# FFT, expert feed-forward and top-1 routing on one core: gates moved from the token loop to the expert tiles

## The chip, the cores and the metric

The kernel runs on 1 core of one Trainium2 chip. The metric is the device time of one execution in microseconds (us), a median over runs.

## What is computed

```python
def reference(x, w1, w2, w3, w_out, expert_emb, tau, e_w1, e_w2):
    X = np.fft.fft(np.fft.fft(x, axis=1), axis=2).real      # x: 8 x 3072 x 256
    t = X.reshape(8 * 3072, 256)
    t = ((t @ w1) * (t @ w2)) @ w3 @ w_out                   # 256 -> 1024 -> 256
    tn = t / (norm(t) + 1e-6)
    logits = tn @ (emb / (norm(emb) + 1e-6)).T / tau         # 8 experts
    e = argmax(logits)
    p = exp(logits - max(logits)); p /= p.sum() + 1e-9
    out[token] = p[e] * (relu(t @ e_w1[e]) @ e_w2[e])        # the chosen expert only
```

p[e] is the gate. At the maximum the exponential is 1, so the gate is one over the sum of the exponentials.

## The kernel before

All matrix products are made from high and low halves: `split` (L110) writes the high half with a ScalarE copy and the low half as source minus high half, on VectorE or GpSimd; three products of halves stand for one. Names with h and l at the end (`jh`, `jl`; `eh`, `el`; `hh`, `hl`) are such halves.

The program has three stretches. The first (to about 315 us) makes the transform of x and folds the constant matrices. The second, `mid` (L714), runs over 24 chunks of 512 columns, each column standing for two tokens (sum and difference), 1024 tokens a chunk; a 25th round is the tail. A chunk has eight steps i. In a step, `stage_b` (L767) makes one block of 128 features of the running chunk c: 13 matmuls of 128x512 into the PSUM tiles `p` and `q`, then the copies and elementwise products `ps`, `a`, `b`, `g`. `just` (L801) splits one block of 128 tokens of the chunk before into `jh` (ScalarE) and `jl` (GpSimd), and `stage_c` (L808) makes its 24 matmuls of 128x264 into one PSUM tile `pc`: 256 features and 8 logits. There is one `pc`; ScalarE copies it into the chunk's row tile `xs` (L815), and the next block's first matmul waits for that copy. After it ScalarE squares and sums the 256 features (L817, tile `jk`).

In step 1 `choose` (L822) works on the eight blocks of the chunk before that one: maximum, the square root of the sum of squares by shifts and three rounds of reciprocal and two multiply-adds (`norm_of`, L127), difference `df`, argmin `mi`, one-hot `oh`, the exponential `ex` on ScalarE (L851), and then the gate and the token number into the row's columns 256 and 257 (L855, L856), over the logits:

```python
        nc.scalar.activation(out=ex, in_=df, func=AF.Exp)
        nc.vector.reciprocal(out=xs[:, 0:nt, D], in_=su)
        nc.vector.tensor_copy(xs[:, 0:nt, D + 1].bitcast(I32), tok[:, t0:t0 + nt])
```

In step 2 `place` ranks the tokens by expert with matmuls, and from step 3 on `scatter` (L879) writes each block's rows of 258 words into the DRAM array `dx`, ordered by expert, with an indirect DMA that GpSimd issues. In every second step `presplit` (L887) takes one of 64 pieces of the experts' weights: SyncE loads `et`, ScalarE and VectorE split it, SyncE stores `eh` and `el` to DRAM; its pool has two buffers for each tile. The next chunk's columns `ru` and `rv` are split in step 5 (`uh`, `ul`, `vh`, `vl`).

The third stretch, `experts` (L1111), runs over up to 103 tiles of 256 rows of `dx`; 100 are sure to run. `turn` transposes a tile into `xh`, `xl`; `up` makes four hidden blocks `pd` and splits them (`hh` on ScalarE L1087, `hl` on VectorE L1088); `down` and `gated` (L1093) make two output blocks `po`, scale them by the gate in the row (`o`, L1102, ScalarE) and scatter them to the token's row of the output (GpSimd, L1103). The first tile is made in the tail, in pieces between the last blocks (`lead_tiles`). A scheduler places the instructions of each engine within a stretch; in `experts` SyncE's order is the program's.

Of the kernel before, what the change touches and what calls it, by code (L numbers as in the profile page):

```python
# [8 lines left out]
F32 = mybir.dt.float32  # L9
# [15 lines left out]
XW = 258  # L25
# [34 lines left out]
def fourier_experts(  # L60
# [110 lines left out]
    def open_p1():  # L171
# [52 lines left out]
    with ExitStack() as c2:  # L224
        c2.enter_context(tc.manual_schedule(engines={mybir.EngineType.SP}))
        experts(nc, tc, c2, p1["w"], p1["xs"], ident, run, t_g, eg, lead, dx, dex, out)
# [487 lines left out]
def mid(  # L714
# [44 lines left out]
    nc.gpsimd.memset(zrow[:, D + 1:D + 2].bitcast(I32), N)  # L759
# [40 lines left out]

    def just(gt, j, lo_eng=nc.gpsimd):  # L801
# [3 lines left out]
        split(h, l, src, lo_eng=lo_eng)  # L805
        return h, l

    def stage_c(hl, xs, ss, j, tag="c"):  # L808
# [13 lines left out]
    def choose(xs, ss, nt, t0, masked, j0=0):  # L822
        xs, ss = xs[:, j0:j0 + nt], ss[:, j0:j0 + nt]
# [5 lines left out]
        nrm = small("nrm", 1)[:, :nt]  # L829
        norm_of(nrm, ss[:, :nt], ro, 128, nt, f"n{nt}")  # L830
        nc.vector.tensor_scalar_add(nrm, nrm, 1e-6)
        inv = small("inv", 1)[:, :nt]
        nc.vector.reciprocal(out=inv, in_=nrm)
# [15 lines left out]
        ex = small("ex")[:, :nt]  # L849
        nc.vector.tensor_tensor(out=df, in0=df, in1=inv.unsqueeze(2).to_broadcast(sh), op=ALU.mult)  # L850
        nc.scalar.activation(out=ex, in_=df, func=AF.Exp)  # L851
        su = small("su", 1)[:, :nt]
# [34 lines left out]
    def presplit(n):  # L887
# [7 lines left out]
        split(h, l, t)  # L895
# [36 lines left out]
    def mini_out(hl):  # L932
        xs = xsp.tile([128, 8, 264], F32, tag="xs", name="xsm")
        ss = ro.tile([128, 8], F32, tag="ss", name="ssm")
        stage_c(hl, xs, ss, 0)
        idx = place(*choose(xs, ss, 1, NCH * 8, True))
# [30 lines left out]
    def lead_tiles():  # L967
        w = p1["w"].rearrange("p (a c) -> p a c", c=2048)
        for x in p1["xs"][:INLINE]:
# [3 lines left out]
            transposed(nc, x, identr, ps, h, l)  # L973
            yield
# [6 lines left out]
            for a in range(2):  # L981
                ps = pp.tile([128, D], F32, tag=f"b{a}", name="lo")
                o = wk.tile([128, D], F32, tag=f"a{a}", name="lout")
                gated(nc, tc, w, hs, a, x, ps, o, out)
# [7 lines left out]
    for c in range(NCH + 1):  # L992
# [5 lines left out]
        if gprev is not None:  # L998
            lo_eng = nc.gpsimd if c < NCH else nc.vector
            if c == NCH:  # L1000
                w0 = p1["w"].rearrange("p (a c) -> p a c", c=2048)
                p1["xs"] = [p1["x"][:, 0:2, :], p1["x"][:, 2:4, :]] + [
                    p1["raw"].tile([128, 2, XW], F32R, tag=t, name="xl") for t in ("ru", "rv")
                ]
                for g, t in enumerate(p1["xs"]):
                    nc.sync.dma_start(
                        out=t.bitcast(F32),
# [5 lines left out]
            xs = xsp.tile([128, 8, 264], F32, tag="xs", name="xs")  # L1013
            ss = ro.tile([128, 8], F32, tag="ss", name="ss")
        masked = (c - 2) % (H // CH) == 0
        for i in range(8):
            if c < NCH:
# [6 lines left out]
                late = (hl, xs, ss, i) if gprev is not None else None  # L1024
                if c == 1 and i == 1:
                    mini_out(hm)
                if pend is not None:
                    if i == CHOOSE:
                        sel = choose(*pend, 8, (c - 2) * 8, masked)
# [29 lines left out]
        pend = (xs, ss) if gprev is not None else None  # L1059
# [33 lines left out]
def gated(nc, tc, w, hs, a, x, ps, o, out):  # L1093
# [3 lines left out]
    for f in range(FT):  # L1097
# [13 lines left out]
def experts(nc, tc, ctx, w0, x0, ident, run, t_g, eg, lead, dx, dex, out):  # L1111
# [6 lines left out]
    xp = pool("xx", LOOK + 2)  # L1118
    wp = pool("xw", 1)
# [20 lines left out]
    nc.gpsimd.memset(zrow[:, D + 1:D + 2].bitcast(I32), N)  # L1140
# [29 lines left out]
    def load_x(g):  # L1170
        r = nc.sync.value_load(entry(1, g), min_val=0, max_val=ROWS - TS)
        t = xp.tile([128, 2, XW], F32R, tag="x", name="x")
        nc.sync.dma_start(out=t.bitcast(F32), in_=dx[bass.ds(r, TS), :].rearrange("(a p) c -> p a c", p=128))
        return t

    xts, ths = {}, {}

    def turn(p):
# [3 lines left out]
        ths[p] = (h, l)  # L1182

# [46 lines left out]
    def table(a, b):  # L1230
        n = b - a
        sh = [1, n, E]
        cm = cp.tile(sh, F32, name=f"cm{a}")
# [9 lines left out]
        rw = cp.tile([1, n], F32, name=f"rw{a}")  # L1243
# [6 lines left out]
        ch = cp.tile([1, n], F32, name=f"ch{a}")  # L1250
# [154 lines left out]
```

## Time and profile before

| | us |
|---|---|
| three runs | 2750.07, 2757.14, 2759.6 |
| median | 2757.14 |
| the profiled execution | 2768.9 |
| its span | 2767.2 |
| its mean granted TensorE clock | 0.976 |
| PE, PEld, DVE busy | 2602.1, 2441.5, 1690.8 |
| ACT, POOL busy | 1049.5, 1078.0 |

The profile names the engines PE (TensorE's matmuls), PEld (its weight loads), DVE (VectorE), ACT (ScalarE), POOL (GpSimd) and SP (SyncE). Shares over the whole span mix the three stretches: VectorE's 1690.8 us lie mostly in the first two, and from about 1610 us on it is busy under a third of the time. So a stretch is looked at by itself, cut where a chunk's first copy of `p` stands in ScalarE's rows. The profiled execution lies 11.8 us above the median of the runs.

### The profile page before, as it was taken

What the parts mean: (1) busy time and instruction counts of PE and PEld (TensorE: products, weight loads), DVE (VectorE), ACT (ScalarE), POOL (GpSimd) and SP (SyncE); (2) the same over time, 40 slices, a digit from 0 to 9 for tenths busy, and PEclk for the clock granted to TensorE, in tenths of its full rate; (3) what the DMA queues carried; (4) which work ended last, traced back from release to release, by engine and by line L of the source; (5) the groups of instructions that cost most, each with busy time, mean ns of one, the idle gap of its engine ahead of it and who ended that gap; (6) DMA issues with size and microseconds to landing.
All of it is one profiled execution on the core that took longest, in us unless ns stands there. A gap on an engine that the chain in (4) does not pass through costs nothing.

```text
span 2767.2 us, 48866 instructions
## 1 busy us (share of the span) xinstructions
PE 2602.1 (94%) x18661; PEld 2441.5 (88%) x18661; DVE 1690.8 (61%) x3325; ACT 1049.5 (38%) x2069; POOL 1078.0 (39%) x748
## 2 busy tenths in 40 slices
PE   4988789999999999999999999999999999999998
PEld 3888677877888888888888899999999999999998
DVE  8999389999888878888888852222222222222222
ACT  3554234444434334434344433333333333333332
POOL 5465345565566555565565421111111111111111
PEclk7999899999999999999999999999999999999999
DMA  6766625455211011011010264111111422111110
GB/s 247 242 220 201 199 92 184 164 173 191 73 41 41 28 43 39 28 43 39 28 43 20 108 267 169 47 47 47 47 47 47 163 104 104 47 47 47 47 47 21
DMA packets 114249, 265.07 MB, mean 96 GB/s; under 512 B 16843, under 2 KB 55929, under 8 KB 109148
## 3 DMA queue, kind: packets, MB, share of 16 engines
q1 hardware_dynamic: 84670, 195.58, 21.5%
q0 software_dynamic: 19440, 51.35, 5.2%
q10 hardware_dynamic: 9902, 14.98, 1.5%
q8 instruction: 148, 2.42, 0.4%
q14 instruction: 89, 0.73, 0.1%
HBM read 521.17 MB, written 106.77 MB: 227 GB/s over the span
## 4 chain that ended last, share of the span: by engine, by line
issue 39%; PE 27%; DVE 17%; POOL 11%; DMA 3%; ACT 2%; POOLq 0%; SPq 0%; DVEq 0%; ACTq 0%
PE pc L122 14%; POOL out L1103 7%; PE p L122 6%; PE q L122 5%; DVE b L796 2%; DVE g L799 2%; POOL vl L115 2%; DMA et<-in 2%; DVE a L796 2%; PE acc L122 1%; DVE ps L781 1%; DVE el L115 1%; ACT jh L112 1%; DVE nrm L139 1%; POOL z L504 1%
## 5 line engine op out<-in xcount | busy, mean ns | idle before, releaser
L1088 DVE SCALAR_TENSOR_TENSOR hl<-pd,hh 128x512 fp32r<-128x512 f32 x396 | 273.8, 691 | 783.5 <-ACT hh L1087 752.6
L115 POOL TENSOR_TENSOR jl<-g,jh 128x1024 fp32r<-128x1024 f32 x184 | 443.0, 2409 | 393.9 <-ACT jh L112 330.2
L1103 POOL DMA_INDIRECT out<-o,x x192 | 187.3, 976 | 916.0 <-ACT o L1102 897.2
L122 PE MATMUL pc<-wh,jh 128*128 128x264 f32 x1536 | 449.9, 293 | 53.1 <-ACT xs L815 50.4
L122 PE MATMUL pc<-wh,jl 128*128 128x264 f32 x1536 | 444.1, 289 | 4.1 <-POOL jl L115 4.0
L122 PE MATMUL pc<-wl,jh 128*128 128x264 f32 x1536 | 442.7, 288 | 0.0
L1084 PE MATMUL pd<-xh,wt 128*128 128x256 f32 x2400 | 431.4, 278 | 0.0
L1100 PE MATMUL po<-wt,hh 128*128 128x256 f32 x2400 | 423.9, 280 | 0.0
L112 ACT ACTIVATE jh<-g 128x1024 fp32r<-128x1024 f32 x192 | 203.2, 1059 | 476.4 <-PE pc L122 350.7
L1084 PEld LDWEIGHTS pd<-xh,wt 128*128 128x128 f32 x2400 | 370.0, 188 | 0.0
L122 PEld LDWEIGHTS pc<-wh,jh 128*128 128x128 f32 x1536 | 296.4, 193 | 82.4 <-ACT xs L815 73.3
L1087 ACT ACTIVATE hh<-pd 128x512 fp32r<-128x512 f32 x396 | 236.7, 598 | 339.8 <-PE pd L1084 339.8
L1100 PEld LDWEIGHTS po<-wt,hh 128*128 128x128 f32 x2400 | 364.4, 188 | 0.0
L1100 PE MATMUL po<-wt,hl 128*128 128x256 f32 x1200 | 334.1, 278 | 0.0
L1084 PE MATMUL pd<-xl,wt 128*128 128x256 f32 x1200 | 333.9, 278 | 0.0
L122 PE MATMUL q<-vh,wc 128*128 128x512 f32 x768 | 308.0, 403 | 17.2 <-ACT a L794 10.6
L122 PE MATMUL p<-uh,wc 128*128 128x512 f32 x768 | 308.1, 402 | 3.7 <-DVE ps L781 3.6
L122 PEld LDWEIGHTS pc<-wl,jh 128*128 128x128 f32 x1536 | 296.9, 193 | 5.8
L122 PEld LDWEIGHTS pc<-wh,jl 128*128 128x128 f32 x1536 | 295.9, 193 | 5.6 <-POOL jl L115 5.4
L796 DVE TENSOR_TENSOR b<-ps,q 128x512 f32<-128x512 f32 x384 | 249.0, 688 | 33.9 <-ACT ps L785 20.3
L880 POOL DMA_INDIRECT dx<-xs,idx x192 | 192.5, 1003 | 154.3 <-DVE idx L876 82.0
L799 DVE TENSOR_TENSOR g<-a,b 128x512 f32<-128x512 f32 x384 | 247.6, 679 | 7.7 <-POOL a L796 7.5
(336 smaller groups left out, 5073.4 us busy)
## 6 DMA issues: line engine op xcount, KB each, us to landing
wt<-dex SPq DMA_DIRECT2D x75, 4096.0 KB
wc<-dex SPq DMA_DIRECT2D x22, 4096.0 KB
x<-dx SPq DMA_DIRECT2D x96, 258.0 KB
xt<-in SPq DMA_DIRECT2D x24, 1028.0 KB
et<-in SPq DMA_DIRECT2D x64, 256.0 KB
dex<-eh SPq DMA_DIRECT2D x64, 256.0 KB
dex<-el SPq DMA_DIRECT2D x64, 256.0 KB
raw<-in SPq DMA_DIRECT2D x28, 512.0 KB
```

The source lines that it names most:

```text
L112: nc.scalar.activation(out=hi, in_=src, func=AF.Copy)
L115: (lo_eng or nc.vector).tensor_tensor(out=lo, in0=src, in1=hi.bitcast(F32), op=ALU.subtract)
L122: nc.tensor.matmul(ps, lhsT=lh, rhs=rh, start=first and i == 0, stop=last and i == n - 1)
L139: nc.vector.scalar_tensor_tensor(out=n_, in0=n_, scalar=0.5, in1=t, op0=ALU.mult, op1=ALU.add)
L796: eng.tensor_tensor(out=t, in0=ps, in1=q, op=o)
L799: nc.vector.tensor_tensor(out=gt[sg][:, f, :], in0=ab[0][sg], in1=ab[1][sg], op=ALU.mult)
L880: i = nc.gpsimd.indirect_dma_start(out=dx, out_offset=bass.IndirectOffsetOnAxis(ap=idx[:, j if k is None else k:][:, 0:1], axis=0), in_=xs ...
L1084: nc.tensor.matmul(ps[:, a, :], lhsT=w[:, lh, o:o + 128], rhs=rh[:, k, :], start=i == 0, stop=i == 5)
L1087: nc.scalar.activation(out=hh[:, sl, :], in_=ps, func=AF.Relu)
L1088: nc.vector.scalar_tensor_tensor(out=hl[:, sl, :], in0=ps, scalar=0.0, in1=hh[:, sl, :].bitcast(F32), op0=ALU.max, op1=ALU.subtract)
L1100: nc.tensor.matmul(ps, lhsT=lh[:, f, sl], rhs=w[:, rh, c:c + D], start=i == 0, stop=i == 3 * FT - 1)
L1103: ins = nc.gpsimd.indirect_dma_start(out=out, out_offset=bass.IndirectOffsetOnAxis(ap=x[:, a, D + 1:D + 2].bitcast(U32), axis=0), in_=o, i ...
```

## The change

The scattered row keeps the logits. It grows from 258 to 265 words: 256 features, 8 logits, and the token number in word 264 (`TK`). The squares leave `stage_c`; the norm, the exponential and the gate leave `choose`. The token number is written by one operation that reads `mi` (always above -1, so the comparison adds 0). A new function `gates` computes a tile's gates from the rows in `turn` (and for the first tile in `lead_tiles`), and `gated` scales by its result. `presplit`'s low half goes to GpSimd. Each scatter is issued behind the `jl` of its step. `table` gives its temporary tiles common tags.

```diff
-XW = 258
+XW = 265
+XP = 272
+TK = 264
...
+    low = [None]
     def just(gt, j, lo_eng=nc.gpsimd):
-        split(h, l, src, lo_eng=lo_eng)
+        low[0] = split(h, l, src, lo_eng=lo_eng).ins
...
-        nc.scalar.activation(out=xs[:, j, :], in_=pc, func=AF.Copy)
-        jk = wk.tile([128, D], F32, tag="jk", name="jk")
-        nc.scalar.activation(out=jk, in_=xs[:, j, 0:D], func=AF.Square, accum_out=ss[:, j:j + 1])
+        nc.scalar.activation(out=xs[:, j, 0:TK], in_=pc, func=AF.Copy)
...
-        norm_of(nrm, ss[:, :nt], ro, 128, nt, f"n{nt}")
-        nc.vector.tensor_scalar_add(nrm, nrm, 1e-6)
-        nc.vector.reciprocal(out=inv, in_=nrm)
...
-        nc.vector.tensor_tensor(out=df, in0=df, in1=inv.unsqueeze(2).to_broadcast(sh), op=ALU.mult)
-        nc.scalar.activation(out=ex, in_=df, func=AF.Exp)
-        nc.vector.tensor_reduce(out=su, in_=ex, axis=AX.X, op=ALU.add)
-        nc.vector.tensor_scalar_add(su, su, 1e-9)
-        nc.vector.reciprocal(out=xs[:, 0:nt, D], in_=su)
-        nc.vector.tensor_copy(xs[:, 0:nt, D + 1].bitcast(I32), tok[:, t0:t0 + nt])
+        nc.vector.scalar_tensor_tensor(
+            out=xs[:, 0:nt, TK].bitcast(I32), in0=mi, scalar=-1.0, in1=tok[:, t0:t0 + nt],
+            op0=ALU.is_lt, op1=ALU.add
+        )
...
-        split(h, l, t)
+        split(h, l, t, lo_eng=nc.gpsimd)
...
-                            scatter(pend[0], idx, j)
+                            with tc.issue_after(low[0]):
+                                scatter(pend, idx, j)
...
+def gates(nc, pool, junk, x, norm_of):
+    sh = [128, 2, E]
+    new = lambda nm, *w: pool.tile([128, *w], F32, tag="g" + nm, name="g" + nm)
+    ss, nrm, mx, inv, gate = (new(nm, 2) for nm in ("ss", "nrm", "mx", "inv", "gate"))
+    for a in range(2):
+        nc.scalar.activation(out=junk, in_=x[:, a, 0:D].bitcast(F32), func=AF.Square, accum_out=ss[:, a:a + 1])
+    lg = x[:, :, D:D + E].bitcast(F32)
+    nc.vector.tensor_reduce(out=mx, in_=lg, axis=AX.X, op=ALU.max)
+    norm_of(nrm, ss, pool, 128, 2, "gn")
+    nc.vector.tensor_scalar_add(nrm, nrm, 1e-6)
+    nc.vector.reciprocal(out=inv, in_=nrm)
+    df = new("df", 2, E)
+    nc.vector.tensor_tensor(out=df, in0=lg, in1=mx.unsqueeze(2).to_broadcast(sh), op=ALU.subtract)
+    nc.vector.tensor_tensor(out=df, in0=df, in1=inv.unsqueeze(2).to_broadcast(sh), op=ALU.mult)
+    ex = new("ex", 2, E)
+    nc.scalar.activation(out=ex, in_=df, func=AF.Exp)
+    nc.vector.tensor_reduce(out=gate, in_=ex, axis=AX.X, op=ALU.add)
+    nc.vector.tensor_scalar_add(gate, gate, 1e-9)
+    nc.vector.reciprocal(out=gate, in_=gate)
+    return gate
...
-    nc.scalar.activation(out=o, in_=ps, func=AF.Copy, scale=x[:, a, D:D + 1].bitcast(F32))
+    nc.scalar.activation(out=o, in_=ps, func=AF.Copy, scale=gate[:, a:a + 1])
...
+    gtp = pool("xg", 3)
...
         ths[p] = (h, l)
+        gts[p] = gates(nc, gtp, ip.tile([128, D], F32, tag="jk", name="jk"), xts[p], norm_of)
...
-        cm = cp.tile(sh, F32, name=f"cm{a}")
+        cm = cp.tile(sh, F32, tag="cm", name=f"cm{a}")
```

The scheduler orders the engines anew. In GpSimd's order of chunk 2, before (`jl` are the low halves of the token blocks, `dx` the scatters, `ul` and `vl` those of the next chunk's columns):

```order
L115 TENSOR_TENSOR ul<-ru,uh 128x512
L115 TENSOR_TENSOR vl<-rv,vh 128x512
L115 TENSOR_TENSOR jl<-g_3570,jh 128x1024 x4
L880 DMA dx<-xs,idx 198912x258 x4
L115 TENSOR_TENSOR jl<-g_3571,jh 128x1024
L880 DMA dx<-xs,idx 198912x258 x4
L115 TENSOR_TENSOR jl<-g_3571,jh 128x1024 x3
```

and now, with `el` the low halves of the experts' weights:

```order
L117 TENSOR_TENSOR jl<-g_3570,jh 128x1024
L117 TENSOR_TENSOR el<-et,eh 128x512 x2
L117 TENSOR_TENSOR jl<-g_3570,jh 128x1024
L873 DMA dx<-xs,idx 198912x265 x2
L117 TENSOR_TENSOR el<-et,eh 128x512 x2
L117 TENSOR_TENSOR jl<-g_3571,jh 128x1024
L873 DMA dx<-xs,idx 198912x265 x2
L117 TENSOR_TENSOR el<-et,eh 128x512 x2
L117 TENSOR_TENSOR jl<-g_3571,jh 128x1024
L873 DMA dx<-xs,idx 198912x265
L117 TENSOR_TENSOR el<-et,eh 128x512
L117 TENSOR_TENSOR jl<-g_3571,jh 128x1024
```

The scatters stand one or two behind each `jl` instead of four in a row (seven in most later chunks), and two `el` stand ahead of most `jl`.

SyncE's order of the weight pieces in the chunks 1 and 2, before (`et` the loads, `dex` the stores):

```order
L897 DMA dex<-el 128x512
L892 DMA et<-in 128x512
L896 DMA dex<-eh 128x512
L897 DMA dex<-el 128x512
L892 DMA et<-in 128x512
L897 DMA dex<-el 128x512
L892 DMA et<-in 128x512
L896 DMA dex<-eh 128x512 x2
L897 DMA dex<-el 128x512
```

and now:

```order
L885 DMA et<-in 128x512 x2
L889 DMA dex<-eh 128x512
L890 DMA dex<-el 128x512
L889 DMA dex<-eh 128x512
L890 DMA dex<-el 128x512
L885 DMA et<-in 128x512 x2
L889 DMA dex<-eh 128x512
L890 DMA dex<-el 128x512
L889 DMA dex<-eh 128x512
L890 DMA dex<-el 128x512
L885 DMA et<-in 128x512 x2
```

Before, loads and stores alternate. Now two loads stand together, behind the four stores of the pair ahead. The pieces come earlier, too: ScalarE's `eh` stood at 5, 7, 9, 10, 10, 10, 10 and 3 in the chunks 0 to 7, and now stand at 8, 14, 14, 14 and 14 in the chunks 0 to 4.

VectorE's order for one expert tile had four `hl` and then `xl`. It is now:

```order
L1093 TENSOR_REDUCE gmx<-x 128x2
L1098 TENSOR_TENSOR gdf<-x,gmx 128x16
L1081 SCALAR_TENSOR_TENSOR hl<-pd,hh 128x512
L131 TENSOR_SCALAR gnh<-gss 128x2
L134 TENSOR_SCALAR gnrm<-gnh 128x2
L139 RECIPROCAL gnq<-gnrm 128x2
L140 SCALAR_TENSOR_TENSOR gnq<-gnq,gss 128x2
L1081 SCALAR_TENSOR_TENSOR hl<-pd,hh 128x512
L141 SCALAR_TENSOR_TENSOR gnrm<-gnrm,gnq 128x2
L139 RECIPROCAL gnq<-gnrm 128x2
L140 SCALAR_TENSOR_TENSOR gnq<-gnq,gss 128x2
L141 SCALAR_TENSOR_TENSOR gnrm<-gnrm,gnq 128x2
```

The small operations stand between the four `hl`, up to five together, and three behind `xl`. On ScalarE a tile's order was `hh` four times, `xh`, `o`, `o`; it is now `jk`, `hh`, `jk`, `hh` three times, `xh`, `gex`, `o`, `o`.

## Rows read from the trace of the kernel before

**Rows 1.** Windows, core 0: us, busy us of each engine (instructions), PEclk, DMA share, GB/s.

```profile
358.10:584.00 225.90, 205.47 (x1216) 179.03 (x1215) 207.75 (x389) 100.02 (x210) 117.56 (x68) 0.95 0.48 157
584.00:1512.70 928.70, 883.81 (x5491) 783.52 (x5490) 780.85 (x1578) 381.60 (x795) 532.17 (x323) 0.99 0.17 56
1512.70:1610.00 97.30, 90.51 (x659) 84.27 (x657) 76.43 (x252) 39.67 (x89) 45.98 (x36) 0.98 0.24 89
1610.00:2767.20 1157.20, 1144.29 (x9876) 1143.68 (x9874) 341.33 (x560) 377.89 (x691) 193.75 (x199) 1.00 0.23 79
```

**Rows 2.** TensorE's timeline (start us, duration us): the first `p` of two successive steps.

```profile
1000.04 0.40 PE L122 MATMUL p<-uh,wc 128*128 128x512 f32 x1
...
1005.95 0.40 PE L122 MATMUL p<-uh,wc 128*128 128x512 f32 x1
```

**Rows 3.** Waits, 584.0 to 1512.7 us: us in total, times, longest.

```profile
ACT jh L112 <- PE q L122: 73.3, 14, 6.5
...
ACT ex L851 <- DVE df L850: 55.2, 18, 4.2
...
PE pc L122 <- ACT xs L815: 38.1, 34, 2.5
...
PE pc L122 <- POOL jl L115: 2.6, 3, 1.4
```

**Rows 4.** TensorE's timeline around one wait for `xs`.

```profile
918.63 0.39 PE L122 MATMUL pc<-wh,jh 128*128 128x264 f32 x1 [2.46 <-ACT xs L815]
...
919.59 0.28 PE L122 MATMUL pc<-wl,jh 128*128 128x264 f32 x1
919.71 0.28 PE L122 MATMUL pc<-wh,jl 128*128 128x264 f32 x1
...
922.41 0.42 PE L122 MATMUL pc<-wh,jh 128*128 128x264 f32 x1
922.63 0.42 PE L122 MATMUL pc<-wl,jh 128*128 128x264 f32 x1
```

**Rows 5.** ScalarE's timeline, the same place.

```profile
918.04 0.26 ACT L851 ACTIVATE ex<-df 128x64 f32<-128x64 f32 x1 [4.17 <-DVE df L850]
```

**Rows 6.** VectorE's timeline, ahead of it.

```profile
914.03 2.34 DVE L139 SCALAR_TENSOR_TENSOR nrm<-nrm,n8q 128x8 f32<-128x8 f32 x1
```

**Rows 7.** GpSimd's timeline, beside it.

```profile
913.95 2.39 POOL L115 TENSOR_TENSOR jl<-g,jh 128x1024 fp32r<-128x1024 f32 x1 [3.48 <-PE p L122]
```

**Rows 8.** Groups by line and shape, whole span; the last one of 1512.7 to 1610.

```profile
L817 ACT ACTIVATE jk<-xs 128x256 f32<-128x256 f32 x192 | 80.0, 417 | 5.3
L115 DVE TENSOR_TENSOR el<-et,eh 128x512 fp32r<-128x512 f32 x64 | 67.9, 1065 | 15.0 <-ACT eh L112 15.0
L112 ACT ACTIVATE eh<-et 128x512 fp32r<-128x512 f32 x64 | 40.1, 630 | 107.3 <-DMA et<-in 59.0 <-issue 8.8 <-DVE g L799 7.5
L817 ACT ACTIVATION_READ_ACCUMULATOR jk<-xs 128x1 f32 x192 | 35.9, 187 | 0.0
L115 POOL TENSOR_TENSOR ul<-ru,uh 128x512 fp32r<-128x512 f32 x24 | 32.5, 1355 | 8.2 <-ACT uh L112 8.2
...
L139 DVE SCALAR_TENSOR_TENSOR nrm<-nrm,n2q 128x2 f32<-128x2 f32 x6 | 0.9, 158 | 0.0
```

**Rows 9.** GpSimd's timeline, one of several scatters in a row.

```profile
922.19 0.98 POOL L880 DMA_INDIRECT dx<-xs,idx  x1 [0.30 <-issue]
```

**Rows 10.** SyncE's timeline, the issue of one store.

```profile
410.30 0.33 SPq L897 DMA_DIRECT2D dex<-el  x1
```

**Rows 11.** Chain of waits, 420 to 520 us, two loads that stand on it.

```profile
420.78 4.57 DMA et<-in
...
436.10 3.31 DMA et<-in
```

**Rows 12.** GpSimd's timeline, the first scatter behind chunk 23.

```profile
1575.64 0.98 POOL L880 DMA_INDIRECT dx<-xs,idx  x1 [15.19 <-DVE xs L855]
```

**Rows 13.** VectorE's timeline in the experts, one `hl`.

```profile
2509.76 0.69 DVE L1088 SCALAR_TENSOR_TENSOR hl<-pd,hh 128x512 fp32r<-128x512 f32 x1 [0.67 <-ACT hh L1087]
```

More of the change, by code (lines that the diff above doesn't have):

```diff
@@ L225, in fourier_experts @@
         c2.enter_context(tc.manual_schedule(engines={mybir.EngineType.SP}))
-        experts(nc, tc, c2, p1["w"], p1["xs"], ident, run, t_g, eg, lead, dx, dex, out)
+        experts(nc, tc, c2, norm_of, p1["w"], p1["xs"], ident, run, t_g, eg, lead, dx, dex, out)
     left2.close()
@@ L932, in mini_out @@
     def mini_out(hl):
[L933 to L936, printed above, removed]
+        xs = xsp.tile([128, 8, XW], F32, tag="xs", name="xsm")
+        stage_c(hl, xs, 0)
+        idx = place(*choose(xs, 1, NCH * 8, True))
         scatter(xs, idx, 0)
@@ L973, in lead_tiles @@
             transposed(nc, x, identr, ps, h, l)
+            gate = gates(nc, ro, wk.tile([128, D], F32, tag="jk", name="jk"), x, norm_of)
             yield
@@ L983, in lead_tiles @@
                 o = wk.tile([128, D], F32, tag=f"a{a}", name="lout")
-                gated(nc, tc, w, hs, a, x, ps, o, out)
+                gated(nc, tc, w, hs, a, x, gate, ps, o, out)
                 yield
@@ L1002, in mid @@
                 p1["xs"] = [p1["x"][:, 0:2, :], p1["x"][:, 2:4, :]] + [
-                    p1["raw"].tile([128, 2, XW], F32R, tag=t, name="xl") for t in ("ru", "rv")
+                    p1["raw"].tile([128, 2, XP], F32R, tag=t, name="xl") for t in ("ru", "rv")
                 ]
@@ L1023, in mid @@
                     stage_c(*late)
-                late = (hl, xs, ss, i) if gprev is not None else None
+                late = (hl, xs, i) if gprev is not None else None
                 if c == 1 and i == 1:
@@ L1058, in mid @@
             first = choose_lead()
-        pend = (xs, ss) if gprev is not None else None
+        pend = xs if gprev is not None else None
         gprev = gt
@@ L1090, in hidden, with gated @@
     )
-def gated(nc, tc, w, hs, a, x, ps, o, out):
+def gates(nc, pool, junk, x, norm_of):
[18 more added lines that the diff above has]
+    return gate
+def gated(nc, tc, w, hs, a, x, gate, ps, o, out):
     hh, hl = hs
@@ L1108, in gated, with experts @@
     tc.add_to_no_dep_group("outs", ins)
-def experts(nc, tc, ctx, w0, x0, ident, run, t_g, eg, lead, dx, dex, out):
+def experts(nc, tc, ctx, norm_of, w0, x0, ident, run, t_g, eg, lead, dx, dex, out):
     pool = lambda nm, n, **k: ctx.enter_context(tc.tile_pool(name=nm, bufs=n, reuse_waits="tile", **k))
@@ L1171, in load_x @@
         r = nc.sync.value_load(entry(1, g), min_val=0, max_val=ROWS - TS)
[L1172 to L1173 removed]
+        t = xp.tile([128, 2, XP], F32R, tag="x", name="x")
+        nc.sync.dma_start(out=t[:, :, 0:XW].bitcast(F32), in_=dx[bass.ds(r, TS), :].rearrange("(a p) c -> p a c", p=128))
         return t
[L1176 removed]
+    xts, ths, gts = {}, {}, {}
     def turn(p):
@@ L1193, in down @@
     def down(p, hs):
-        x = xts.pop(p)
+        x, gate = xts.pop(p), gts.pop(p)
         for a in range(2):
@@ L1197, in down @@
             o = op.tile([128, D], F32, tag=f"o{a}", name=f"o{a}")
-            gated(nc, tc, wt[seq[p] // STRL % NSTR], hs, a, x, ps[:, 0:D], o, out)
+            gated(nc, tc, wt[seq[p] // STRL % NSTR], hs, a, x, gate, ps[:, 0:D], o, out)
     nxt_of = {}
```

45 lines of the change are left out of this document (20 added, 25 removed).

## The prediction

> **What bounds the kernel now.** Begin with the table of stretches [rows 1], cut at chunk starts. From 1610 us to the end (the experts) TensorE is busy 1144 of 1157 us at full clock, while VectorE works 341 us and ScalarE 378 us: this stretch is as long as its matmuls, and work added to the other engines is free there as long as it makes no matmul wait. The middle stretch is different. Its 18 chunks from 584.0 to 1512.7 us take 928.7 us, 51.6 us each, but an undisturbed step lasts 5.91 us [rows 2], so eight of them are 47.2 us, and with about 0.3 us for the rank matmuls a chunk needs 47.5 us. 4.1 us per chunk, 74 us in the 18, are lost.
>
> The waits say where [rows 3]: TensorE waits 38.1 us for ScalarE's copy `xs`, almost its only large wait, and ScalarE waits 18 times, once in every chunk and 55.2 us in all, in front of the exponential `ex` for VectorE's `df`. One instance shows both [rows 4, 5]. `ex` starts at 918.04 after 4.17 us of waiting; `xs` stands behind it in ScalarE's order, and the stage-C matmul, which needs the single PSUM tile that `xs` empties, starts only at 918.63 after 2.46 us of idleness. Then the spacing of the matmuls goes from 0.12 us (919.59 to 919.71) to 0.22 us (922.41 to 922.63): the granted clock fell to the lower of its two levels, 1.2 GHz, and about 14 matmuls cost 0.10 us more each, 1.4 us. The pause and its echo make nearly the whole 4.1 us: 38.1/18 = 2.1 us of waits and about 1.4 us of slow clock; the next largest of TensorE's waits, for `jl`, is 2.6 us in all [rows 3], 0.14 us a chunk.
>
> Why is `df` late? It ends a chain of small VectorE operations for the norm, fourteen of the seventeen that the gate takes. One of them, on 128x8 elements, starts at 914.03 and ends at 916.37, 2.34 us [rows 6]; GpSimd's `jl` beside it ends at 916.34 [rows 7].
>
> **The change part by part.**
>
> *Norm and gate leave the middle stretch.* Per chunk, `ex`, eight squares on ScalarE (417 ns each and 187 for the read-out [rows 8]) and those seventeen VectorE operations go. What remains of the choice (maximum, difference, argmin, one-hot, token number, then ranks) asks nothing of ScalarE, so nothing there stands ahead of `xs` but `jh`, which is ready in time in the undisturbed steps. I take 48.3 us per chunk after the change, 0.8 us above the clean 47.5, for the small waits and half a microsecond of something late once per chunk. 18 x (51.6 - 48.3) = 59 us less. Bounds: 0.2 us left over (-70 us); 2.5 us left, if something else is late next in half the chunks (-29 us). I stay near the first because TensorE has no second wait of that size in this stretch [rows 3].
>
> *64 low halves `el` move from VectorE to GpSimd.* On VectorE they average 1065 ns, waits included; GpSimd's `ul`, same shape and operation, takes 1355 ns [rows 8]. The Trainium skill (GPSIMD Engine Reference, 4.1 Engine selection) says the opposite of this edit: two-input elementwise work belongs to VectorE, GpSimd being about half as fast. The trace agrees on the pace (1.36 against 1.07 us here, waits on VectorE included), but by that rule alone the move would cost 64 x 0.29 = 19 us, and the sum below would be 19 us higher; I don't count it, since GpSimd's load is not what sets the step. The load of a full chunk: 14 x 1.36 + 8 x 2.4 (`jl` [rows 7]) + 8 x 1.28 (a scatter and the gap before it [rows 9]) + 2 x 1.36 = 51 us.
>
> What sets the step is a loop. The scheduler now packs the preparation into pairs: 8 in chunk 0, then 14 in each of the chunks 1 to 4 (before: about 10 per chunk, until chunk 7). In SyncE's new order both loads of the next pair stand behind both stores of this one, so they start only when the second `el` is done. One turn: 0.33 us for the store's issue [rows 10], 3.31 to 4.57 us until a load has landed [rows 11], 0.63 us for `eh` [rows 8], twice 1.36 us for `el`: 7.0 to 8.3 us, more than the step's 5.91. I take 7.4, nearer the short end, because the chain of waits, from which [rows 11] come, picks the late loads. 28 pairs x 7.4 + 4 lone steps x 5.9 = 231 us for the chunks 1 to 4, against 225.9 now [rows 1]: +5 us, from -6 (7.0) to +30 (8.3). Chunk 0 holds 3 more splits in front of GpSimd's `a`: +3 us, 0 to +10.
>
> *Scatters.* Each goes behind the `jl` of its step instead of seven in a row. Their cover is GpSimd's idle time in late chunks (2.41 + 2.6 us of 5.91 per step); if that is gone, as in the chunks 1 to 4, `jl` is late next, but the loop above is longer still. Nothing more is counted. Rows of 1060 instead of 1032 bytes: 2.7% of transfers that nobody waits for; nothing.
>
> *Chunk 23 and the hand-over*, 97.3 us [rows 1]: one pause less (-3 us); the first scatter after it waited at the end for the gate's reciprocal (L855) on VectorE [rows 12], and goes some 3 us earlier; against this the gates of the first tiles stand among the index tables on VectorE, +1 us. -5 us, from -9 to +2.
>
> *Gates per tile in the experts.* Two squares with read-out (2 x 0.6 us), one Exp and nineteen VectorE operations on 128x2 or 128x16, near 0.16 us each (158 ns [rows 8]). Per tile (11.6 us) that is 1.5 us on ScalarE, busy 33%, and about 3 us on VectorE, busy 29%. In VectorE's order four to five small operations stand between two `hl`, 0.4 to 0.6 us when they follow each other at 0.1 us, and the idle gap there is 0.67 us [rows 13]. `df` is finished ahead of the fourth `hl` in VectorE's new order, so `ex` finds it ready on a ScalarE that is idle two thirds of the time. Cover is this idle time; without it, 3 PSUM tiles `pd` still let VectorE lag. 0 us, up to +12.
>
> **The sum.** -59 + 5 + 3 - 5 + 0 = -56 us. The profiled execution took 2768.9 us (span 2767.2), 11.8 above the median of the runs; so 2713 on its terms and 2757.1 - 56 = **2701 us** for the median. Own range of this case 2682 to 2735.
>
> **The rivals.**
>
> 1. *The pair loop is slow and pulls the clock down.* At 8.3 us per turn TensorE pauses 2.4 us in 28 steps, as long as the pause in [rows 4]; with 1.4 us of low clock each, 39 us come on top of +25: 2765 us. For it: the loads of `et` stand on the chain of waits already [rows 11], and the chunks 1 to 4 have a mean clock of 0.95 [rows 1]. Against it: at 7.4 us the pause is 1.5 us, and the shorter pauses that make up the 38.1 us [rows 3] left the mean clock of the 18 chunks at 0.99 [rows 1]. The Trainium skill (TensorE: Matmul & The Clock Gate, HAM oscillation) describes this pattern, a pause for data in each round that returns the clock to half rate; here only single pauses show it so far. Chance 0.13, split over faster (short version, 2735), same and slower.
>
> 2. *Half of the late chunks' loss stays*, because another wait comes in front of `xs` or `jl`: -29 instead of -59 us, 2731 us. For it: 14 times `jh`, which also stands ahead of `xs`, waits for a matmul `q` of the running chunk, 73.3 us in all [rows 3], and the change does not touch that. Against it: those waits fall into time in which TensorE is busy. Chance 0.12.
>
> 3. *The gate chain holds the experts up*, and the kernel is slower. Place: ScalarE's order, `ex` in front of the two `o`. It decides if the small operations take more than about 0.4 us each: then fourteen of them outlast the three gaps of 0.67 us between the `hl` plus the two spare `pd` tiles (2.8 us), and every tile grows. One microsecond each in 97 tiles: 2701 + 97 = 2798 us. For it: such an operation took 2.34 us beside `jl` [rows 6]. Against it: in the experts GpSimd runs scatters only, and in the hand-over, where scatters run too, the 128x2 shape took 158 ns [rows 8]. Chance 0.06.
>
> 4. *Everything lands at the good end* (late chunks clean, loop at 7.0): about 2680 us. Chance 0.07.
>
> That the change doesn't do what it says is excluded by the new order of instructions, which shows the squares, `ex` and `el` gone from their old places.
>
> **How the numbers follow.** Forecast 0.62, rivals 0.13, 0.12, 0.06, 0.07. Within 0.3% is about what a measurement of this kernel can tell from no change: 2749 to 2765 us. Faster: 0.62 + 0.12 + 0.07 and a few hundredths of rival 1, less what spills over 2749: 0.83. Same 0.07, slower 0.10. The range 2676 to 2745 leaves out the far ends of rivals 1 and 4 and all of rival 3.
>
> **What would show it.** Right: no `ex` wait on ScalarE in the middle stretch, TensorE's wait for `xs` far below 38 us there, late chunks of 48 to 49 us, chunks 1 to 4 near 57 us with SyncE and ScalarE waiting for `el` and `et`, experts still at 11.6 us per tile with TensorE without idleness. Wrong: late chunks above 50 us; chunks 1 to 4 above 62 us with clock below 0.9; any idle time of TensorE in the experts.

## The result and the profile after

The changed kernel takes 2707.14 us (2705.4 to 2711.13, four runs), the kernel before 2754.26 us beside it: a ratio of 0.9831, 95% interval 0.9815 to 0.9846, 47 us less. The profiled execution of after has a span of 2703.6 us, that of before had 2767.2, so between the two profiles there are 63.6 us to account for. The stretches of after, cut as in [rows 1] (columns as there):

```profile
0.00:307.60 307.60, 236.88 (x1273) 218.42 (x1273) 257.81 (x498) 136.59 (x261) 154.93 (x107) 0.92 0.71 237
307.60:352.90 45.30, 39.94 (x152) 31.46 (x153) 26.70 (x49) 16.41 (x32) 33.08 (x27) 0.77 0.53 171
352.90:590.10 237.20, 206.42 (x1219) 176.21 (x1218) 172.00 (x281) 94.51 (x160) 184.63 (x124) 0.97 0.63 213
590.10:1445.90 855.80, 855.80 (x5492) 777.32 (x5491) 718.95 (x1250) 297.00 (x468) 536.43 (x323) 1.00 0.12 40
1445.90:1543.20 97.30, 88.57 (x639) 83.33 (x637) 65.20 (x177) 30.64 (x53) 43.84 (x35) 0.96 0.24 89
1543.20:2703.60 1160.40, 1148.82 (x9892) 1148.21 (x9892) 584.97 (x2448) 469.29 (x1188) 194.68 (x199) 1.00 0.24 80
```

The fourth row is the gain. The 18 late chunks took 928.7 us and take 855.8, 47.5 each, and TensorE is busy in every one of those microseconds. Of the 72.9 us less, 44.9 were idleness (928.70 - 883.81) and 28.0 a longer busy time for the same matmuls (883.81 against 855.80 us). The lower clock is only a part of these 28: in this stretch of the kernel before the granted clock stood at half in six places, 20.5 us in all, which costs 10.2 us; in after it never did. The waits of this stretch (us, times, longest) begin so, and no row of TensorE is among them, where [rows 3] had 38.1 us:

```profile
ACT jh L114 <- PE pc L124: 403.5, 144, 3.2
POOL jl L117 <- ACT jh L114: 237.0, 114, 3.5
```

The 38.1 us of [rows 3] carry one name, but they are two pauses. Rows of three engines in one chunk of the kernel before, in order of time:

```profile
968.92 0.26 ACT L851 ACTIVATE ex<-df 128x64 f32<-128x64 f32 x1 [2.57 <-DVE df L850]
...
969.51 0.39 PE L122 MATMUL pc<-wh,jh 128*128 128x264 f32 x1 [0.82 <-ACT xs L815]
...
979.50 0.98 POOL L880 DMA_INDIRECT dx<-xs,idx  x1 [0.30 <-issue]
...
982.15 1.06 ACT L112 ACTIVATE jh<-g 128x1024 fp32r<-128x1024 f32 x1 [6.48 <-PE q L122]
983.12 0.37 ACT L815 ACTIVATE xs<-pc 128x264 f32<-128x264 f32 x1
...
983.54 0.39 PE L122 MATMUL pc<-wh,jh 128*128 128x264 f32 x1 [1.84 <-ACT xs L815]
```

The first pause is the one behind `ex`. The second comes 14 us later: the scatter shown is the last of a row of seven, a late `jh` starts behind that row, and `xs` stands behind `jh`. Of the 34 waits for `xs`, 15 (18.8 us) have `ex` right ahead of `xs`, one in each of the chunks 8 to 22. Another 12 (14.7 us) follow a late `jh`, 1.8 to 3.1 us behind the end of a scatter row. The other 7 (4.6 us) lie in the chunks 5 to 7. The two pauses of a chunk share their cost: where the first is 0.8 to 0.9 us long (ten chunks), the second is 0.67 to 1.84; where the first is 1.76 to 2.46 (five chunks), the second is at most 0.35.

The chunks 1 to 4 (third row) lost 11.3 us. The timeline of after in chunk 2 shows the pair loop whole (start us, duration us):

```profile
441.74 1.28 ACT L114 ACTIVATE eh<-et 128x512 fp32r<-128x512 f32 x2 [4.57 <-DMA et<-in]
...
443.91 2.55 POOL L117 TENSOR_TENSOR el<-et,eh 128x512 fp32r<-128x512 f32 x2
...
446.49 0.33 SPq L890 DMA_DIRECT2D dex<-el  x1
446.91 0.90 SPq L885 DMA_DIRECT2D et<-in  x2
450.44 0.63 ACT L114 ACTIVATE eh<-et 128x512 fp32r<-128x512 f32 x1 [5.71 <-DMA et<-in]
```

Splits, then the store of the second `el`, then the loads, then the next `eh` 8.7 us after the last. The hand-over, from chunk 23's first copy to the first full expert matmul `pd`, grew from 94.7 to 98.1 us. TensorE's waits in it went from 6.0 to 9.4 us: 3.8 for `xs` are gone, 3.6 for `wrx` and 1.1 for `xh` are new, and the wait for `ohot` grew by 2.5. The two largest of after:

```profile
PE pr L856 <- DVE ohot L841: 3.6, 1, 3.6
PE lt L1063 <- DMA wrx<-dx: 3.6, 1, 3.6
```

The load of the lead tile's rows `wrx` is issued behind the last scatter of chunk 23, in after 45.6 us into that chunk:

```profile
1488.84 0.99 POOL L873 DMA_INDIRECT dx<-xs,idx  x1
...
1491.54 1.08 SPq L999 DMA_DIRECT2D wrx<-dx  x2
```

and in the kernel before, where that chunk began at 1512.7, 37.5 us:

```profile
1547.58 0.99 POOL L880 DMA_INDIRECT dx<-xs,idx  x1 [0.17 <-PE q L122]
...
1550.17 9.49 SPq L1006 DMA_DIRECT2D wrx<-dx  x2
```

From the first `pd` to the last `po` it is 1149.2 us before and 1149.0 after. That is a sum of two parts. The first ten tiles took 126.9 us and take 122.6; a wait of 2.1 us for a load of `x` is no longer there. The other 89 took 1022.0 us and take 1026.1, 0.05 us more each. The runs below agree: with the old gates these 89 tiles take 1022.0 us in four of five profiles (1019.6 in the fifth), with the new ones 1025.9 to 1026.8 in all seven. Of the groups by line and shape of after (count, then busy us and mean ns), the low halves of the weights on GpSimd, over the whole span, and the commonest of the gates' small operations, from 1700 to 2690 us:

```profile
L117 POOL TENSOR_TENSOR el<-et,eh 128x512 fp32r<-128x512 f32 x64 | 81.7, 1292 | 41.8 <-ACT eh L114 41.7
...
L141 DVE SCALAR_TENSOR_TENSOR gnrm<-gnrm,gnq 128x2 f32<-128x2 f32 x251 | 39.6, 158 | 5.8
```

### The profile page after: what moved, and what is told of

It is laid out like the page before. It is cut to its first block, busy times and chain, and to the rows that moved or that the text cites. A ratio compares the mean times of both kernels' runs of the same rounds, so it can differ in the third digit from the quotient of the medians.

```text
span 2703.6 us, 50360 instructions
## 1 busy us (share of the span) xinstructions
PE 2576.4 (95%) x18661; PEld 2435.0 (90%) x18661; DVE 1825.6 (68%) x4702; ACT 1044.4 (39%) x2156; POOL 1147.6 (42%) x812
## 4 chain that ended last, share of the span: by engine, by line
issue 36%; PE 35%; POOL 8%; DMA 1%; POOLq 0%; ACT 0%; DVE 0%; SPq 0%; ACTq 0%
PE pc L124 18%; PE p L124 9%; PE q L124 8%; POOL out L1118 7%; DMA et<-in 1%; POOLq L1118 0%; POOL el L117 0%; PE ld L1077 0%; POOL jl L117 0%; PE pr L858 0%; ACT jh L114 0%; POOL dx L873 0%; DMA wrx<-dx 0%; ACT eh L114 0%; DVE b L798 0%
## 5 line engine op out<-in xcount | busy, mean ns | idle before, releaser
L1118 POOL DMA_INDIRECT out<-o,x x192 | 187.8, 978 | 919.9 <-ACT o L1117 901.4
L124 PE MATMUL pc<-wh,jh 128*128 128x264 f32 x1536 | 440.8, 287 | 17.3 <-ACT xs L819 14.4
L1115 PE MATMUL po<-wt,hh 128*128 128x256 f32 x2400 | 434.0, 283 | 0.0
L124 PE MATMUL q<-vh,wc 128*128 128x512 f32 x768 | 305.3, 399 | 13.3 <-ACT a L796 11.3
L1117 ACT ACTIVATE o<-po,ggate 128x256 f32<-128x256 f32 x198 | 94.2, 476 | 418.6 <-PE po L1115 418.6
```

The lines of the kernel that those rows point to most:

```text
L124: nc.tensor.matmul(ps, lhsT=lh, rhs=rh, start=first and i == 0, stop=last and i == n - 1)
L1115: nc.tensor.matmul(ps, lhsT=lh[:, f, sl], rhs=w[:, rh, c:c + D], start=i == 0, stop=i == 3 * FT - 1)
L1117: nc.scalar.activation(out=o, in_=ps, func=AF.Copy, scale=gate[:, a:a + 1])
L1118: ins = nc.gpsimd.indirect_dma_start(out=out, out_offset=bass.IndirectOffsetOnAxis(ap=x[:, a, TK:TK + 1].bitcast(U32), axis=0), in_=o, in_ ...
```

## The experiments

Each run's profile was cut in the same way, at the first copy of `p` of each chunk in ScalarE's rows; "lead" is the time from the start of chunk 23 to the first matmul `lt` of the lead tile, "hand-over" to the first `pd`. All in us; the median stands beside that of the kernel before on the same chip.

| kernel | median (before) | first stretch | chunks 1-4 | 5-6 | 7-22, each | lead | hand-over | experts |
|---|---|---|---|---|---|---|---|---|
| before | 2754.3 | 315.2 | 225.9 | 109.0 | 51.2 | 49.9 | 94.7 | 1149.2 |
| before, again | 2756.8 | 311.8 | 222.9 | 110.1 | 51.0 | 49.8 | 94.3 | 1145.1 |
| ex behind xs | 2767.2 (2756.6) | 308.2 | 222.5 | 108.3 | 51.5 | 49.3 | 93.8 | 1149.0 |
| scatter edge only | 2753.4 (2759.3) | 314.0 | 229.6 | 112.1 | 49.8 | 53.0 | 97.7 | 1148.8 |
| both queues | 2725.7 (2759.3) | 307.8 | 230.3 | 110.1 | 48.2 | 51.8 | 99.4 | 1148.6 |
| gates only | 2749.0 (2756.6) | 308.4 | 229.0 | 108.4 | 49.6 | 54.3 | 102.3 | 1149.1 |
| after, no scatter edge | 2769.6 (2756.6) | 310.7 | 253.0 | 98.8 | 49.6 | 53.1 | 101.1 | 1148.8 |
| after, el on VectorE | 2702.8 (2759.3) | 307.8 | 226.1 | 103.9 | 47.5 | 48.7 | 99.1 | 1148.8 |
| after | 2707.1 (2754.3) | 307.6 | 237.2 | 95.0 | 47.5 | 48.7 | 98.1 | 1149.0 |
| after, spread | 2687.9 (2759.3) | 311.9 | 207.0 | 97.3 | 48.2 | 45.6 | 94.6 | 1149.0 |
| spread, eh behind jh | 2665.9 (2758.0) | 312.3 | 197.8 | 95.1 | 47.5 | 45.5 | 93.7 | 1149.5 |
| after, gates twice | 2715.4 (2758.0) | 308.7 | 238.0 | 95.1 | 47.5 | 48.8 | 100.2 | 1154.7 |

**The kernel before, again.**

> The kernel before, unchanged, profiled a second time. The profile of before had a first stretch of 315.2 us, the profile of after 307.6 us, and the change touches nothing there. Theory: this 7.6 us is variation from run to run, so this profile has a first stretch near 308 us, 18 late chunks near 51.6 us each again, and a span of 2750 to 2757 us. Rival: the rest of the profiled execution's surplus of 12 us lay in the late chunks; then the first stretch is again near 315 us and the late chunks come out below 51.2 us each.

The result lies in between. The span is 2755.0 us; of the 12.2 us less than in the first profile, 3.4 lie in the first stretch, 3.5 in the 18 late chunks (51.4 each) and 4.1 in the experts. Over all the profiles the first stretch varies from 307.6 to 315.2 us, with no relation to the edits, so 7.6 of the 63.6 us are variation. Against this second profile the changed kernel gains 51.4 us, near the 47 of the medians.

**The exponential behind the copy, in the kernel before.**

```diff
-        nc.scalar.activation(out=ex, in_=df, func=AF.Exp)
...
+                        with tc.issue_after(copied[0]):
+                            wait[0]()
```

(`copied` holds the step's copy `xs`; `wait[0]` is the exponential and the operations behind it.)

> The kernel before with one edge of order: the exponential ex stands right behind the copy xs of its step on ScalarE instead of right ahead of it, and the gate's last operations are written a step later. Squares, norm chain, scatters and el stay. Theory (the late chunks lost their 4.1 us because xs stood behind ex): TensorE's wait for xs falls from 38 us to under 10 us in the late chunks, these take about 48 us instead of 51.6, and the kernel comes out near 2754 - 60 = 2694 us, at most 2715. Rival (the norm chain and the squares load VectorE and ScalarE, and something else is late next, jh or ps behind ex): late chunks stay at 50 us or more, 2725 us or above.

The rival is right: 2767.2 us, ratio 1.004 (1.0024 to 1.0055). The wait for `xs` did fall, as the theory said, and another took its place. Waits, 575.5 to 1507.2 us:

```profile
POOL dx L889 <- DVE xs L859: 60.7, 17, 4.8
...
PE pc L122 <- POOL jl L115: 37.3, 18, 2.7
...
PE pc L122 <- ACT xs L817: 3.4, 5, 1.1
```

The pause behind `ex` is gone, and the one at the end of the scatter row has grown by as much: TensorE is idle for 45.7 us of the 18 chunks, 44.9 before.

GpSimd's timeline in one chunk shows why `jl` is late: seven scatters stand ahead of it, the first of which had to wait for the gate.

```profile
965.33 0.98 POOL L889 DMA_INDIRECT dx<-xs,idx  x1 [3.02 <-DVE xs L859]
...
973.03 0.98 POOL L889 DMA_INDIRECT dx<-xs,idx  x1 [0.30 <-issue]
974.02 2.37 POOL L115 TENSOR_TENSOR jl<-g,jh 128x1024 fp32r<-128x1024 f32 x1
```

**Gates moved, the other two parts undone.**

```diff
-        split(h, l, t, lo_eng=nc.gpsimd)
+        split(h, l, t)
...
-                            with tc.issue_after(low[0]):
-                                scatter(pend, idx, j)
+                            scatter(pend, idx, j)
```

> The changed kernel with two of its parts undone: el back on VectorE, scatters without the edge behind jl; the gates stay in the expert tiles. Theory: the late chunks are as clean as in the changed kernel (47.5 us each), because moving the gates alone did that. The hand-over gets back the 3.4 us it lost, since the scatters end some 7 us earlier in the last chunk. The weight pieces stand at 12 in each of the chunks 2 to 5; chunks 1 to 6 together 325 to 340 us against 332 in the changed kernel. In all 2695 to 2712 us. Rival (scatters behind jl, or el on GpSimd, did part of the work): late chunks of 49 us or more, 2725 us or above.

The rival again: 2749.0 us, ratio 0.9974 (0.9961 to 0.9987). No `ex` is left on ScalarE in the middle stretch, and the late chunks still lose 2 us each. The 18 of them take 901.4 us, 24 to 27 less than in the two profiles of before; the hand-over takes 8 more and the chunks 1 to 4 take 3 to 6 more. GpSimd's timeline in one of them:

```profile
956.38 0.99 POOL L873 DMA_INDIRECT dx<-xs,idx  x1 [0.99 <-DVE idx L869]
...
965.41 0.98 POOL L873 DMA_INDIRECT dx<-xs,idx  x1 [0.30 <-issue]
966.39 4.76 POOL L117 TENSOR_TENSOR jl<-g,jh 128x1024 fp32r<-128x1024 f32 x2
```

Eight scatters hold GpSimd for 10 us, nearly two steps, and two `jl` follow at once, both late. ScalarE's `jh` is late, too: it starts as the row ends (966.39), and `xs` is queued behind it. TensorE waits for that `xs` and then for the first of the two `jl` (rows of ScalarE and TensorE):

```profile
966.45 1.06 ACT L114 ACTIVATE jh<-g 128x1024 fp32r<-128x1024 f32 x1 [5.41 <-PE p L124]
...
967.41 0.37 ACT L819 ACTIVATE xs<-pc 128x264 f32<-128x264 f32 x1
...
967.84 0.39 PE L124 MATMUL pc<-wh,jh 128*128 128x264 f32 x1 [0.88 <-ACT xs L819]
968.07 0.28 PE L124 MATMUL pc<-wl,jh 128*128 128x264 f32 x1
968.83 0.39 PE L124 MATMUL pc<-wh,jl 128*128 128x264 f32 x1 [0.49 <-POOL jl L117]
```

In 14 of the 16 chunks 7 to 22 `jh` starts within 0.1 us of the row's end. The trace puts its wait down to TensorE's matmuls; what ties it to the end of the row is not shown.

The hand-over didn't shrink either (102.3 us); TensorE waits for `xs` there as well (8.3 us in all).

**The changed kernel without the scatter edge.** The second half of the diff above, alone.

> The changed kernel without the edge that puts each scatter behind jl; el stays on GpSimd. Theory: eight scatters in a row fit into GpSimd's idle time, the late chunks stay at 47.5 us, and the lead tile's load no longer comes 7 us late, so the hand-over is 3 us shorter: 2704 us. Rival: eight scatters in a row (about 10 us) hold up jl, TensorE waits for jl, late chunks above 48.5 us and the kernel slower by 15 us or more, 2722 us or above.

The rival: 2769.6 us, ratio 1.0052 (1.0039 to 1.0066). Without this one edge the change would have made the kernel slower. The late chunks are those of the kernel with the gates alone; the chunks 1 to 4, where `el` shares GpSimd with the scatter row, take 253.0 us.

**The scatter edge alone, in the kernel before.**

```diff
+                            with tc.issue_after(low[0]):
-                            scatter(pend[0], idx, j)
+                                scatter(pend[0], idx, j)
```

> The kernel before with one part of the change alone: each scatter queues behind the jl of its step on GpSimd; gates, squares and el as before. The runs so far show two queues that each hold up TensorE at the same place of a chunk: xs behind ex on ScalarE, and jl behind a row of scatters on GpSimd. Theory (the two pauses overlap, so that mending one alone brings little): late chunks 50.0 to 51.3 us against 51.3, TensorE's wait for xs still near 36 us, 2735 to 2757 us in all. Rival (the scatter row alone is worth its 2 us per chunk): late chunks near 49.3 us, 2720 us.

The time is the theory's (2753.4 us, ratio 0.9972, 0.9962 to 0.9981), and so are the 18 chunks with 50.5 us each, but its reason isn't: the wait for `xs` is 26.6 us, not near 36. The 15 pauses behind `ex` are all still there, with the 18.8 us that they had, and those at the end of a row are gone. So in the late chunks this edge is worth something by itself: the 18 take 908.2 us, 20.5 and 17.0 less than in the two profiles of before. The chunks 1 to 4 (4 to 7 us more) and the hand-over (3 more) take back 7 to 10. The waits (588.2 to 1496.4 us):

```profile
ACT ex L853 <- DVE df L852: 55.3, 18, 4.2
PE pc L122 <- ACT xs L817: 26.6, 24, 2.5
```

**Both queues mended, no gate moved.** The edits of `ex` behind `xs` and of the scatter edge together.

> The kernel before with both queues mended and no gate moved: ex right behind xs on ScalarE, and each scatter behind the jl of its step on GpSimd. Squares, the norm chain and el stay. Theory: both pauses are gone, late chunks 47.5 to 48.5 us, waits of TensorE for xs and jl below 10 us each, 2754 - 18 x 3.3 = 2695 us, at most 2705; the move of the gates into the expert tiles is then worth next to nothing of its own. Rival (the squares, or the norm chain beside jl on the other engine, cost time too): late chunks 49 us or more, 2722 us or above.

Neither side fully: the pauses are gone (the wait for `xs` is 7.1 us, none for `jl` is listed), but the 18 chunks take 48.9 us each, and the time is the rival's, 2725.7 us, ratio 0.9877 (0.986 to 0.9893). Against the kernel with the gates moved and `el` on VectorE (the next run), which differs in the gates and what goes with them (squares, norm, longer rows), 0.6 us per chunk remains in the chunks 7 to 22 (10 us), some 10 us in the chunks 1 to 6. So the gates' move is worth 21 us between these two profiles (spans of 2723.0 and 2702.0 us), once the queues are in order.

**The low half back on VectorE.** The first half of the diff of the gates-only kernel, alone.

> The changed kernel with one part undone: el back on VectorE. Theory: late chunks unchanged at 47.5 us; the pair loop is shorter by some 1 us per pair and the pieces stand at 12 per chunk over the chunks 2 to 5, so the chunks 1 to 6, 332 us in the changed kernel, take 318 to 330 us; 2693 to 2706 us. Rival (VectorE is the bound of the early chunks, el on it costs more than on GpSimd): chunks 1 to 6 of 335 us or more, 2710 us or above.

As the theory had it, at its upper end: 2702.8 us, ratio 0.9793 (0.9777 to 0.9809); chunks 1 to 6 take 330.0 us against 332.2. So `el` on GpSimd costs 1.6 us by the two spans, 4 by the medians and 10 by the ratios to the runs of before beside each; the intervals of the ratios don't overlap.

**Pieces spread, scatters of the last chunk in pairs.**

```diff
+                        with tc.issue_after(low[0]):
+                            presplit(n)
...
-                        if PLACE + 1 + j * (7 - PLACE) // 8 == i:
+                        if PLACE + 1 + (j * (7 - PLACE) // 8 if c < NCH - 1 else j // 2) == i:
```

> The changed kernel with two edits. Each weight piece is traced behind the jl of its step, so that the scheduler leaves four in a chunk up to chunk 15 and doesn't pack them into pairs; and in the last chunk of the loop the scatters go two behind each jl of the steps 3 to 6, so that they end some 5 us earlier. Theory (the chunks 1 to 4 are bound by the loop load, eh, el, store over two buffers; the lead tile's load waits for the last scatter): chunks 1 to 4 near 50 us each and 200 us together, against 237; the chunks 5 to 15 stay below 48 us; the first matmul of the lead tile 45 us into the last chunk's window instead of 48.7; in all 2707 - 37 - 3 = 2667 us. Rival (GpSimd or ScalarE have no room for a piece every second step without making jl or xs late): chunks 1 to 15 of 49 us or more, 2690 us or above.

Neither side fully: 2687.9 us, ratio 0.9741 (0.9719 to 0.9763). The chunks 1 to 4 fell to 207.0 us and the lead tile starts 45.6 us into its window, 3.1 earlier, with the hand-over 3.5 shorter: the load did wait for the last scatter. But the chunks 5 to 14 took 48.9 us each. Their cause is a split `eh` placed too early, as the next run shows (waits, 561.4 to 1429.2 us):

```profile
ACT eh L114 <- DMA et<-in: 155.5, 36, 5.9
...
PE pc L124 <- ACT xs L819: 8.5, 18, 0.9
```

**And eh behind jh.**

```diff
-                        with tc.issue_after(low[0]):
+                        with tc.issue_after(high[0]), tc.issue_after(low[0]):
                             presplit(n)
```

> The kernel with the spread weight pieces and the pairs of scatters in the last chunk, with one edit more: each piece's eh is traced behind the jh of its step on ScalarE, as its el already is behind jl on GpSimd. In the spread kernel the scheduler put eh a step too early: ScalarE waited 144.5 us, 34 times, for the load et in the chunks 5 to 14, with jh queued behind, and TensorE then waited for xs; these chunks took 48.9 us instead of 47.5. Theory: eh now finds its piece loaded, ScalarE's wait for et is below 10 us there, and the chunks 2 to 15 go at 47.6 us like the later ones: 2688 - 14 - 6 = 2668 us. Rival (0.63 us of eh behind xs makes ps late, or el on GpSimd makes jl late): chunks 5 to 15 of 48.5 us or more, 2682 us or above.

The theory, to 2 us: 2665.9 us, ratio 0.9659 (0.9625 to 0.9693), the fastest kernel here, 41 us below the changed one. From chunk 2 to chunk 22 every chunk takes 47.5 us:

```profile
358.20:556.00 197.80, 193.23 (x1217) 173.92 (x1216) 163.35 (x283) 75.43 (x122) 134.94 (x83) 0.99 0.30 97
556.00:1411.80 855.80, 855.80 (x5492) 777.36 (x5491) 724.63 (x1249) 319.63 (x510) 592.37 (x368) 1.00 0.24 80
```

**Gates computed twice.**

```diff
+        for _ in range(2):
-        gts[p] = gates(...)
+            gts[p] = gates(...)
```

> The changed kernel with the gates of every tile computed twice in the experts (the second result is the one used): four squares, two exponentials and 38 small VectorE operations per tile instead of two, one and 19. Theory (the gates lie in idle time of VectorE and ScalarE and cost nothing): VectorE goes from 585 to some 830 us busy of 1160, still below TensorE; the experts stay at 1149 us from the first matmul pd to the last po, within 3 us, and the hand-over, where the first tiles' gates stand among the index tables, grows by 1 to 3 us; 2706 to 2713 us. Rival (between the hl there is room for four to five small operations but not for ten): every tile grows by half a microsecond or more, experts of 1200 us or above, 2755 us or above.

2715.4 us, 8 more than the changed kernel by the medians, and 2.1 of it in the hand-over as expected. The experts took 5.7 us more, over the 3 us allowed: 5.0 in the first 36 us, with a pause of 1.8 us for VectorE's `hl`, and 0.7 much later at a second such pause, of 0.39 us. Elsewhere the tiles go at the pace of the changed kernel, and TensorE is hardly ever idle (1700 to 2700 us of this kernel):

```profile
1700.00:2700.00 1000.00, 999.61 (x8612) 999.41 (x8611) 639.94 (x3637) 480.77 (x1443) 168.28 (x172) 1.00 0.19 62
```

## Why the prediction was right, and where it was not

The forecast was 2701 us, with a range of 2676 to 2745; 2707.1 lies in it, on the side that was forecast. Its sum was -56 us; the medians moved by -47, the two profiles by -63.6. By its steps:

- *Late chunks, -59 us.* Measured -72.9, just past the good bound of -70 (-69.4 against the second profile of before). The half microsecond per chunk that was kept for "something late" isn't there. The idleness was read nearly right (38 us of waits, 44.9 found). The slow clock was not: one instance, 1.4 us, was taken for all 18 chunks, 25 us, and the trace has it in six places, 10.2 us.
- *Why they became clean.* Here the reasoning fell. It laid all the waits for `xs` to `ex` and said that with `ex` gone "nothing there stands ahead of `xs` but `jh`, which is ready in time in the undisturbed steps", and of the scatters "Nothing more is counted". But 12 of these waits, 14.7 us, stood behind a `jh` that was not ready in time, at the end of a row of scatters. So two queues held TensorE up in a chunk, at two places: `xs` behind `ex` on ScalarE, and `jh` and `jl` at the end of a row of seven scatters on GpSimd. Each mended alone brought little in all. The move of `ex` brought nothing (ratio 1.004), since the second pause grew by what the first had cost; the scatter edge 0.3% of the time and the gates' move 0.3%, both with a gain in the late chunks that the hand-over and the early chunks took back in part. The move of `ex` and the edge together brought 33.6 us (1.2%) with nothing else changed. The scatter edge, priced at nothing, decides the sign: without it the changed kernel is slower than before. Rival 2, a second wait in front of `xs` that leaves half of the loss, had the right place: it named `jh`, waiting 73.3 us for `q`. Wrong were its reasons against: these waits did not all "fall into time in which TensorE is busy", and the change does touch them, by the scatter edge.
- *Pair loop, +5 us from -6 to +30.* +11.3. The mean turn by the same sum is (237.2 - 23.6) / 28 = 7.6 us against 7.4, and the loop of SyncE's loads behind the stores is what the timeline shows; spreading the pieces took it away. Rival 1's slow clock did not come: the mean is 0.97, against 0.95 before.
- *`el` on GpSimd.* The move by itself costs 2 to 10 us, not 19. The Trainium skill's rule (GPSIMD Engine Reference, 4.1 Engine selection) that such work belongs on VectorE has the sign right here, by a small amount. GpSimd's `el` takes 1292 ns. VectorE's took 1065 in the mean, with its waits, and 693 in the median, so the pace that the prediction compared, 1.36 against 1.07, made GpSimd look nearer than it is (1292/693 = 1.9).
- *Chunk 0, +3 us.* +2.4 (42.9 to 45.3).
- *Hand-over, -5 us from -9 to +2.* +3.4, outside its bounds. The pause that was to go did go (3.8 us of waits for `xs`). But the step read only the first scatter behind chunk 23; it missed that the edge also moves the scatters inside chunk 23, the last of them from 34.9 to 42.9 us after its start, and that the lead tile's load stands behind them. Two scatters per step, in the run that also spread the pieces, gave it back. Why the rank matmul `pr` waits 3.6 us for `ohot` wasn't tried by itself.
- *Gates in the experts, 0 us.* 1149.2 us before and 1149.0 after, but the nothing is a sum: 4.3 us less in the first ten tiles and 4.1 more in the other 89. What the 0.05 us per tile are wasn't tried; they aren't the small operations' time, since doubling the gates adds nothing to them but one pause of 0.39 us. The small operations took 158 ns, as [rows 8] said.

That the sum came out was luck. Between the two profiles, without the first stretch, the steps add up to -72.9 + 11.3 + 2.4 + 3.4 - 0.2 = -56.0 us, the forecast itself: the late chunks were 13.9 us better than forecast, the pair loop and the hand-over 14.7 worse. And the late chunks came out as they did because what was not seen (the scatters' 2 us per chunk) was part of the change and so part of the gain.

## What to carry to other kernels

A wait list adds up waits by the name of the tile, so one line can hold two pauses with two causes: 34 waits in 18 chunks were a sign of that. Before pricing the removal of a wait, look at several instances, at what stands ahead of the late instruction in its queue each time, and ask when the next operand would have come; a pause that is removed can come back further on. Long runs of instructions on one queue (eight scatters, 10 us) belong behind the step's urgent work, one or two at a time. Once the orders are set by hand, spread background work evenly and place each half of it (here `eh` and `el`) behind the urgent instruction of its own engine: with the last chunk's scatters in pairs that was worth another 41 us.

## What was not expected of the hardware

How little of the cost of a pause was the clock behind it. The pause of 2.46 us in [rows 4] was followed by the lower clock. But over the 18 late chunks of the kernel before the granted clock stood at half in six places only, each at a pause of 1.76 to 2.46 us, and in the second profile of the same kernel in three. That is 10.2 us of the 28.0 by which TensorE was busy longer. In the kernel with the gates alone the pauses are shorter (0.88 and 0.49 us in the chunk shown above); its chunks 7 to 22:

```profile
689.40:1482.40 793.00, 770.32 (x4882) 692.14 (x4881) 635.49 (x1110) 263.18 (x415) 472.56 (x287) 1.00 0.11 37
```

At the pace of the clean chunks (855.80/5492 = 0.1558 us per matmul) 4882 matmuls are 760.7 us, so 9.6 us are lost here beside the 22.7 us of idleness, although the mean granted clock is 1.00. It stood at half in one place, which costs 1.7 us. An estimate for the rest comes from the rows themselves: in [rows 4] a matmul `pc` counts as busy for 0.28 us while the next starts 0.12 us behind it, and the first one behind a pause starts 0.23 us ahead of the next (967.84 and 968.07 above). So a pause costs some 0.16 + 0.11 = 0.27 us more than its idle time tells, and the 30 pauses of these chunks 8.1 us. By the same estimate the 41 pauses of the 18 chunks before are 11 us, and some 7 of the 28.0 remain unexplained.
